# q and k laid out by the host with the dims on the partitions: attention followed by two MLPs

## Chip, core and metric

The kernel runs on one core of a Trainium2 chip, in one launch. The metric is device time in microseconds (us): the time of the run on the chip, as the median of several runs. Engines are named as in the profile: PE is TensorE (matmuls), DVE VectorE, ACT ScalarE, POOL GpSimd, SP the engine that issues most DMAs. Arrays are float32 in the chip's memory (HBM), except the MLP weights, which are float64.

## The reference

B = 4 batches, H = 8 heads, S = 576 positions, D = 64 dims per head. q and k are turned by rope, attention is a full softmax per head, and the result, 2304 tokens of 512, goes through two MLPs.

```python
def rotate(x):                                   # x: [B, H, S, 64]; cos, sin: [S, 32]
    x1, x2 = x[..., :32], x[..., 32:]
    return concatenate([x1 * cos - x2 * sin, x1 * sin + x2 * cos], axis=-1)
scores = matmul(rotate(q), rotate(k).transpose(0, 1, 3, 2)) / sqrt(64)
attn = exp(scores - max(scores)); attn = attn / (sum(attn) + 1e-9)
x = matmul(attn, v).transpose(0, 2, 1, 3).reshape(2304, 512)
x = (sigmoid(x @ w_gate) * (x @ w_val)) @ w_out              # hidden dim 1536
h = x @ w2_in                                                # hidden dim 2048
out = (h * sigmoid(1.702 * h)) @ w2_out
```

## The kernel before

**Pairs, tiles, slots.** Two heads make a pair: 16 pairs, p0 to p15. A head has four tiles of 128 queries and a tail of 64; the two tails share a tile, so a pair has nine units of scores (even units the first head, odd ones the second, the ninth both tails). The program is written out in slots, one unit of scores each (`slot`, from line 586), in a fixed order on every engine. Slot 9i holds the first scores of pair i. Each other stage of a pair comes a fixed number of slots ahead of 9i (`LOAD`, `ROPE_MUL`, `ROPE_ADD`, `ROPE_T`) or behind it (`PT`, `PV`, the normalisation). In a slot the order is: scores, splits left from the slot before (`later`), products with V, transposes of P, loads, normalisation, rope, exponential, a step of weight decoding. Each engine works its own list in order and waits where an operand or a buffer isn't ready.

**q and k.** `load` brings q and k of a pair with the positions on the partitions (x: four positions to a partition, then the tails). Rope multiplies by a sine table with the halves of the dims swapped and by a cosine table (six products on POOL, `rope_mul`), and adds on DVE (`rope_add`). `transpose_qk` turns nine blocks of 128x128 on PE into PSUM, in three groups. Of each group ACT takes a rounded high part X (type float32r, which PE multiplies fast) and DVE the rest Y = x - X. Both are [64 dims of two heads, 1152 columns of q and k]. `stack` then moves halves with six DMAs on SP, so that the high and low parts of one head lie on the 128 partitions: X and Y belong to the first head, Z and Zs to the second. The fifth and sixth of them overwrite what the first four read, so SP waits for those to land. The scores of a unit (`scores`) are two matmuls per half of the keys, which sum the exact products of the parts. p0 does its stacking on ACT and DVE straight from PSUM (`stack_first`).

**After the scores.** DVE takes the row maximum, ACT the exponential and its sum, DVE the reciprocal, POOL multiplies P by it. PE transposes P (41 blocks a pair, `transpose_p`; PSUM tiles of one tag, three buffers, shared with `transpose_qk`), ACT or DVE bring the blocks to SBUF, PE multiplies with V (`pv`), and the result is split into high and low parts for the MLPs. V and P keep the interleaved order of positions, so the output rows come out in runs with a step of four, and `out2` stores each tile with one or more DMAs (`row_runs`), on SP and in the last block partly on POOL.

**The MLPs** follow with all tokens on chip. The float64 weights are decoded to float32 by integer operations on DVE, with one operation on ACT and one on POOL per piece. The first chunk is decoded during the attention, one operation a slot, from unit 4 of p3 on. The later ones go beside the MLP matmuls.

Of the kernel before, what the change touches and what calls it, by code (L numbers as in the profile page):

```python
# [8 lines left out]
F32 = mybir.dt.float32  # L9
# [13 lines left out]
# bits 0x0feffe00: the high word of float32's largest numbers, after the scaling  # L23
# [8 lines left out]
def attention_then_mlps(  # L32
    ctx: ExitStack,
    tc: tile.TileContext,
    q: bass.AP,
    k: bass.AP,
# [6 lines left out]
    cos_t: bass.AP,  # L43
    sin_t: bass.AP,
# [4 lines left out]
    B, H, S, D = q.shape  # L49
    NT, DM = out.shape  # L50
    FF1 = w_gate.shape[1]
# [97 lines left out]
    npairs = B * NPAIR  # L149
# [10 lines left out]
    def load(i):  # L160
        b, hp = divmod(i, NPAIR)
        hs = slice(2 * hp, 2 * hp + 2)
        x = rp.tile([P, 2, NCHK, D], F32, tag="x", name="x", bufs=2)
        # first head: k main | k tail, q tail | q main; second: q main | q tail, k tail | k main
        main = lambda src, h: src[b, h, 0:MAIN, :].rearrange("h (p c) d -> p h (c d)", p=P)
        nc.sync.dma_start(
            out=x.rearrange("p h c d -> p (h c d)")[:, (MAINC + 1) * D : (3 * MAINC + 1) * D].rearrange(
                "p (h n) -> p h n", h=2
            ),
            in_=main(q, hs),  # L170
        )
        for h, c, pq in ((0, 0, TAIL), (1, MAINC + 1, 0)):
            nc.sync.dma_start(
                out=x[:, h : h + 1, c : c + MAINC, :].rearrange("p h c d -> p h (c d)"),
                in_=main(k, slice(2 * hp + h, 2 * hp + h + 1)),
            )
            for src, p in ((q, pq), (k, TAIL - pq)):
                nc.sync.dma_start(out=x[p : p + TAIL, h, MAINC, :], in_=src[b, 2 * hp + h, MAIN:S, :])
        st[i] = dict(x=x, P={})
        st[i]["nm"] = sp.tile([P, 2, 5], F32, tag="nm", name="nm", bufs=4)  # L180
        st[i]["sum"] = sp.tile([P, 9], F32, tag="sum", name="sum", bufs=4)

    def load_v(i):
        b, hp = divmod(i, NPAIR)
        vt = sp.tile([P, 2 * MAINC + 1, D], F32, tag="v", name="v", bufs=3)
        for h in range(2):
            nc.sync.dma_start(out=vt[h * TAIL : (h + 1) * TAIL, 2 * MAINC, :], in_=v[b, 2 * hp + h, MAIN:S, :])
        nc.sync.dma_start(
            out=vt[:, 0 : 2 * MAINC, :].rearrange("p (h c) d -> p h (c d)", h=2),
            in_=v[b, 2 * hp : 2 * hp + 2, 0:MAIN, :].rearrange("h (p c) d -> p h (c d)", p=P),  # L190
        )
        st[i]["v"] = vt

    def rope_mul(i, n, eng=nc.gpsimd):
        x = st[i]["x"]
        if n == 0:
            st[i]["xr"] = rp.tile([P, NCHK, 2, D], F32, tag="xr", name="xr", bufs=2)
        t = st[i]["xr"]
        h, n = divmod(n, 3)
# [12 lines left out]

    def transpose_qk(i, g):
        """q and k with the dims of both heads on the partitions, in exact hi and lo parts; columns
        [k main | k tail | q tail | q main] of the first head, [q main | q tail | k tail | k main]
        of the second."""
        xr = st[i]["xr"]
        if g == 0:
            for n in ("X", "Y", "Z"):
                st[i][n] = rp.tile([P, NCHK * P], F32R, tag=n, name=n, bufs=2)  # L220
            st[i]["Zs"] = rp.tile([P, S], F32R, tag="Zs", name="Zs", bufs=2)
        g0, g1 = ((0, 3), (3, 6), (6, 9))[g]
        ps = ps_t.tile([P, 512], F32, tag="pt", name="ps_qk", bufs=3)
        n = (g1 - g0) * P
        for ch in range(g0, g1):
            nc.tensor.transpose(  # L226
                ps[:, (ch - g0) * P : (ch - g0 + 1) * P], xr[:, ch].rearrange("p h d -> p (h d)"), ident
            )

        c = slice(g0 * P, g1 * P)  # L230
        X, Y, Z, Zs = (st[i][n_] for n_ in ("X", "Y", "Z", "Zs"))

        def split():
            hi, lo = X[:, c], Y[:, c]
            nc.scalar.activation(hi, ps[:, :n], AF.Copy)
            nc.vector.tensor_tensor(lo, ps[:, :n], f(hi), ALU.subtract)
            if g == 2:
                stack(i)

        if i:  # L240
            later.append(split)
        return ps[:, :n], c
# [50 lines left out]
    def exps(i, u):  # L293
        """Rows of P: exp(s - max), unnormalised, and their sums."""
# [31 lines left out]
    # the groups of P transposed that DVE takes out of PSUM, and not ACT; those of the first pair  # L326
# [75 lines left out]
    def split_mm(ps, l, r, n):  # L402
        """Sum of n products of exactly split operands: hi*hi + hi*lo + lo*hi."""
# [29 lines left out]
    row_runs = []  # L433
    for t in range(NT // P):
        runs = []
        c = 0
        while c < P:
            b, j = divmod(t * P + c, S)
            if j < MAIN:
                ch, p0 = divmod(j, P)  # L440
                n = min(P - c, P - p0)
                runs.append((c, n, b * S + MAINC * p0 + ch, MAINC))
            else:
                n = min(P - c, S - j)
                runs.append((c, n, b * S + j, 1))
            c += n
        row_runs.append(runs)

# [23 lines left out]
    def out2(c, nchunk, W, n, g):  # L472
        if c == 0:
            new_acc(n)
        for t in range(width[n] // P):
# [7 lines left out]
            if c == nchunk - 1:  # L483
                for x, (o, m, row, step) in enumerate(row_runs[n * BLK // P + t]):
# [217 lines left out]
```

## Time and profile before

| | |
|---|---|
| time, median of 3 runs | 1165.64 us (1165.47 to 1167.69) |
| span of the profiled execution | 1165.3 us; what lies around the span isn't listed |
| busy: PE, DVE, ACT, POOL | 1134.9, 766.2, 426.1, 327.1 us |
| first matmul of scores | 15.84 us |
| first matmul of an MLP | 323.3 us |
| read from HBM, written to it | 50.46 MB, 4.72 MB |

PE busy means that a matmul is in its pipeline, so matmuls overlap and their own durations add up to more than their share; the chain of waits gives each only what it adds. PEld is PE's weight load, SPq the issue of a DMA by SP. A row with "x3" stands for three instructions merged.

### The profile page before, as it was taken

Reading aid. Unit: us, or ns where it says so; the run is one execution under the profiler, and the core shown is the slowest. Engines: PE = TensorE matmul, PEld = TensorE weight load, DVE = VectorE, ACT = ScalarE, POOL = GpSimd, SP = SyncE. Lnnn points to the kernel's source line nnn. Section 1 sums busy time; section 2 is a strip of 40 time slices with the busy share of each in tenths; the row PEclk is TensorE's granted clock in tenths of the full one; section 3 lists DMA queues with packets and bytes.
Section 4 is the critical chain, followed back from the end, with each engine's and each line's share of the span. In section 5 each row is a group of like instructions: output and inputs, shape, how many; then the busy total and the mean of one; then the engine's idle time right before and its main releaser. Section 6 shows DMA issues by size and latency. Waiting matters only on the chain.

```text
span 1165.3 us, 16369 instructions
## 1 busy us (share of the span) xinstructions
PE 1134.9 (97%) x6096; PEld 917.3 (79%) x6096; DVE 766.2 (66%) x1388; ACT 426.1 (37%) x952; POOL 327.1 (28%) x333
## 2 busy tenths in 40 slices
PE   3999999999999999999999999999999999999998
PEld 2776666777688888888888888888888888888886
DVE  6879999777544555555655555567667676676744
ACT  3776777777621211211212112332323223232221
POOL 6768787765300010100101002331001010010100
PEclk9999999999999999999999999999999999999999
DMA  4555655453211111111111111011111111111014
GB/s 128 123 147 145 150 136 138 110 124 84 66 37 37 37 55 37 55 37 37 55 37 55 37 37 36 20 37 55 37 37 55 37 55 37 37 55 37 19 37 126
DMA packets 46063, 76.15 MB, mean 65 GB/s; under 512 B 11728, under 2 KB 24016, under 8 KB 45984
## 3 DMA queue, kind: packets, MB, share of 16 engines
q1 hardware_dynamic: 45696, 74.19, 23.3%
q8 instruction: 48, 0.79, 0.3%
q0 software_dynamic: 288, 0.92, 0.2%
q14 instruction: 31, 0.25, 0.1%
HBM read 50.46 MB, written 4.72 MB: 47 GB/s over the span
## 4 chain that ended last, share of the span: by engine, by line
PE 90%; DMA 3%; DVE 2%; ACT 2%; issue 1%; SPq 1%; POOL 1%; POOLq 0%; DVEq 0%
PE psh L406 42%; PE pso L406 29%; PE ps_x L377 6%; PE ps_p L347 4%; PE pss L287 3%; PE pss L288 3%; DMA Zs<-X 2%; PE ps_qk L226 1%; DMA X<-Y 1%; ACT P L305 1%; DVE r L318 0%; ACT PT L334 0%; SPq L266 0%; DVE xr L211 0%; DVE nm L290 0%
## 5 line engine op out<-in xcount | busy, mean ns | idle before, releaser
L406 PE MATMUL psh<-xhl,w_in 128*128 128x512 f32 (+1 forms) x2400 | 504.2, 368 | 0.0
L406 PEld LDWEIGHTS psh<-xhl,w_in 128*128 128x128 f32 x2400 | 419.3, 188 | 76.1 <-issue 0.5
L420 ACT ACTIVATE sg<-psh 128x512 f32<-128x512 f32 (+1 forms) x140 | 77.5, 554 | 367.5 <-PE psh L406 366.8
L406 PE MATMUL pso<-w_out,g 128*128 128x512 f32 x864 | 202.4, 389 | 0.0
L422 DVE TENSOR_TENSOR gf<-psh,sg 128x512 f32<-128x512 f32 (+1 forms) x140 | 88.9, 635 | 158.7 <-PE psh L406 111.9
L406 PEld LDWEIGHTS pso<-w_out,g 128*128 128x128 f32 x864 | 161.7, 188 | 33.2
L423 ACT ACTIVATE g<-gf 128x512 fp32r<-128x512 f32 (+1 forms) x140 | 82.5, 590 | 242.0 <-DVE gf L422 242.0
L138 POOL TENSOR_TENSOR w_in<-wt,w_in 128x512 fp32r<-128x512 f32 x40 | 51.7, 1292 | 389.0 <-DVE w_in L137 389.0
L424 DVE TENSOR_TENSOR g<-gf,g 128x512 fp32r<-128x512 f32 (+1 forms) x140 | 95.3, 681 | 91.7 <-ACT g L423 91.7
L406 PE MATMUL pso<-g,w_out 128*128 128x512 f32 (+1 forms) x720 | 152.8, 368 | 0.0
L406 PEld LDWEIGHTS pso<-g,w_out 128*128 128x128 f32 x720 | 125.8, 189 | 22.6
L290 DVE TENSOR_REDUCE nm<-pss 128x1 f32<-128x576 f32 x144 | 108.0, 750 | 49.0 <-PE pss L288 48.3
L322 POOL TENSOR_SCALAR P<-P,r 128x576 f32<-128x576 f32 x128 | 106.4, 844 | 84.9 <-DVE r L319 47.9
L138 POOL TENSOR_TENSOR w_out<-wt,w_out 128x512 fp32r<-128x512 f32 x28 | 36.1, 1290 | 264.0 <-DVE w_out L137 264.0
L377 PE MATMUL ps_x<-PT,v 128*64 128x256 f32 (+3 forms) x640 | 105.3, 425 | 3.3 <-DVE xhl L396 3.3
L305 ACT ACTIVATE P<-pss,nm 128x576 f32<-128x576 f32 x128 | 95.5, 746 | 26.6 <-DVE nm L290 24.6
L334 ACT ACTIVATE PT<-ps_p 128x384 f32<-128x384 f32 (+2 forms) x193 | 77.7, 435 | 59.4 <-PE ps_p L347 43.7
L482 DVE TENSOR_TENSOR acc<-pso,acc 128x512 f32<-128x512 f32 x126 | 83.1, 685 | 20.3 <-PE pso L406 18.0
L347 PE MATMUL ps_p<-ident,P 128*128 128x128 f32 x576 | 84.5, 279 | 1.1 <-POOL P L322 0.9
L347 PEld LDWEIGHTS ps_p<-ident,P 128*128 128x128 f32 x576 | 65.8, 141 | 24.7 <-issue 20.0
L467 DVE TENSOR_TENSOR acc<-pso,acc 128x512 f32<-128x512 f32 (+1 forms) x100 | 61.6, 634 | 28.8 <-PE pso L406 28.8
L377 PEld LDWEIGHTS ps_x<-PT,v 128*64 128x64 f32 (+1 forms) x640 | 35.8, 134 | 31.8 <-issue 20.4
(59 smaller groups left out, 1035.4 us busy)
## 6 DMA issues: line engine op xcount, KB each, us to landing
raw<-in_moe_w_out_dram SPq DMA_DIRECT2D x28, 512.0 KB, 3.5
raw<-in_moe_w_in_dram SPq DMA_DIRECT2D x16, 512.0 KB, 3.6
raw<-in_moe_w_gate_dram SPq DMA_DIRECT2D x12, 512.0 KB, 3.8
raw<-in_moe_w_val_dram SPq DMA_DIRECT2D x12, 512.0 KB, 3.8
Z<-X SPq DMA_DIRECT2D x15, 288.0 KB, 3.1
Z<-Y SPq DMA_DIRECT2D x15, 288.0 KB, 3.9
X<-Y SPq DMA_DIRECT2D x15, 288.0 KB, 3.0
x<-in_q_dram SPq DMA_DIRECT2D x16, 256.0 KB, 3.0
```

The costliest lines, as they stand in the source:

```text
L138: lambda: nc.gpsimd.tensor_tensor(w[:, 1, :], f(t), f(w[:, 0, :]), ALU.subtract),
L290: nc.vector.tensor_reduce(nm, ps[:, :, :HALF], axis=AX.XY, op=ALU.max, negate=True)
L305: nc.scalar.activation(st[i]["P"][j][:, c : c + S].rearrange("p (n c) -> p n c", n=2), ps[:, :, :HALF], AF.Exp, bias=nm, accum_out=st[i][" ...
L322: nc.gpsimd.tensor_scalar(pt, pt, r[:, c - a : c - a + 1], 1.0, op0=ALU.mult, op1=ALU.mult)
L334: nc.scalar.activation(dst, src, AF.Copy)
L347: nc.tensor.transpose(ps[:, t * P : (t + 1) * P], pt[:, (3 * g + t) * P : (3 * g + t + 1) * P], ident)
L377: nc.tensor.matmul(ps[h * D : (h + 1) * D, :n], vt[r, vc, :], PT[r, pc, :], start=(t == 0), stop=(t == MAINC))
L406: nc.tensor.matmul(ps, l(sl, a), r(sr, a), start=(sl == 1 and a == 0), stop=(sl + sr == 0 and a == n - 1))
L422: nc.vector.tensor_tensor(gf, pss[-1][:, :wd], sg, ALU.mult)
L423: nc.scalar.activation(g[:, 0, m, :], gf, AF.Copy)
L424: nc.vector.tensor_tensor(g[:, 1, m, :], gf, f(g[:, 0, m, :]), ALU.subtract)
L482: nc.vector.tensor_tensor(a, ps[:, :DM], a, ALU.add)
```

## The change

The host (where arrays are only laid out, and tables of the shapes alone are made) now gives q and k as one array: per pair 128 partitions (64 dims of the first head, 64 of the second) by 1152 columns, and once more with the two halves of each head's dims swapped. Columns are, for the first head, k main, k tail, q tail, q main, and for the second q main, q tail, k tail, k main: the order that X, Y, Z had. "HALVES" 0 and 1 are the columns 0 to 575 and 576 to 1151. cos and sin come in the same layout, [128, 2, 1152]. v comes in tiles as the kernel holds them. Positions keep their natural order, so each output tile of 128 rows is stored by one DMA. The MLPs don't change.

```diff
-    def load(i):                # 7 DMAs: q main of both heads; per head k main, q tail, k tail
-    def load_v(i):              # 3 DMAs, 3 buffers
-    def rope_mul(i, n, eng=nc.gpsimd):   # 6 per pair: 4 of [128, 9x32], 2 of [128, 9x64]
-    def rope_add(i, h):
-    def transpose_qk(i, g):
-    def stack_first(h):
+    HALVES = (slice(0, S), slice(S, 2 * S))
+    def load(i, c=slice(0, 2 * S)):
+        if i not in st:
+            st[i] = dict(P={}, x=rp.tile([P, 2 * S], F32, tag="x", name="x", bufs=2))
+        nc.sync.dma_start(out=st[i]["x"][:, c], in_=qk[i, 0, :, c])
+    def load_swapped(i, n, c=slice(0, S)):
+        if ("xs", n) not in st[i]:
+            st[i]["xs", n] = rp.tile([P, S], F32, tag="xs", name="xs", bufs=3)
+        nc.sync.dma_start(out=st[i]["xs", n][:, c], in_=qk[i, 1, :, n * S + c.start : n * S + c.stop])
+    def load_v(i):
+        vt = sp.tile([P, 2 * MAINC + 1, D], F32, tag="v", name="v", bufs=2)
+        nc.sync.dma_start(out=vt, in_=v[i])
+    def mul(i, swapped, n, eng, c=slice(0, S)):
+        c_ = slice(n * S + c.start, n * S + c.stop)
+        t = st[i]["xs", n][:, c] if swapped else st[i]["x"][:, c_]
+        eng.tensor_tensor(t, t, cos_sin[:, swapped, c_], ALU.mult)
+    def add(i, n, c=slice(0, S)):
+        x = st[i]["x"][:, n * S + c.start : n * S + c.stop]
+        nc.vector.tensor_tensor(x, x, st[i]["xs", n][:, c], ALU.add)
+    def rope_mul(i, n):
+        mul(i, 1 - n % 2, n // 2, nc.gpsimd)
+    def rope_add(i, n):
+        add(i, n)
+    def split_qk(i, n):
+        if n == 0:
+            new_pair(i)                       # tiles X, Y, Z, Zs, nm, sum
+        c = HALVES[n]
+        x, hi, lo = (st[i][n_][:, c] for n_ in ("x", "X", "Y"))
+        nc.scalar.activation(hi, x, AF.Copy)
+        nc.vector.tensor_tensor(lo, x, f(hi), ALU.subtract)
+        if n == 1:
+            stack(i)
+    def first_pair():
+        k, q = HALVES
+        q0, q1 = slice(S, S + TAIL + P), slice(S + TAIL + P, 2 * S)
+        lo, hi = slice(0, D), slice(D, P)
+        first, others = slice(0, TAIL + P), slice(TAIL + P, S)
+        for c, n, c_ in ((k, 0, slice(0, S)), (q0, 1, first), (q1, 1, others)):
+            load(0, c)
+            nc.scalar.dma_start(out=cos_sin[:, :, c], in_=cos_sin_t[:, :, c])
+            load_swapped(0, n, c_)
+        load(1)
+        load_swapped(1, 0)
+        nc.gpsimd.dma_start(out=ident, in_=ident_t)
         ...
+        def rope(c, n, c_, eng):
+            mul(0, 0, n, nc.vector, c_)
+            mul(0, 1, n, eng, c_)
+            add(0, n, c_)
+            hi_of(X[lo, c], x[lo, c])         # hi_of: ACT copy; rest: DVE subtraction
+        rope(k, 0, slice(0, S), nc.gpsimd)
+        rope(q0, 1, first, nc.vector)
+        rest(X[hi, k], x[lo, k], X[lo, k])
+        hi_of(Y[hi, q0], x[lo, q0])
+        rest(X[hi, q0], x[lo, q0], X[lo, q0])
+        nc.vector.tensor_copy(Y[lo, q0], f(X[hi, q0]))
+        rope(q1, 1, others, nc.gpsimd)
+        hi_of(Zs[hi], x[hi, k])
+        hi_of(Y[hi, k], x[hi, q])
+        hi_of(Z[lo, k], x[hi, k])
+        hi_of(Z[lo, q], x[hi, q])
+        rest(Z[hi, k], x[hi, k], Zs[hi])
+        rest(Z[hi, q], x[hi, q], Y[hi, k])
+        nc.vector.tensor_copy(Zs[lo], f(Z[hi, k]))
+        rest(X[hi, q1], x[lo, q1], X[lo, q1])
+        nc.vector.tensor_copy(Y[lo, q1], f(X[hi, q1]))
+        hi_of(Y[hi, q1], x[lo, q1])
     ...
     def out2(c, nchunk, W, n, g):
         ...
-                for x, (o, m, row, step) in enumerate(row_runs[n * BLK // P + t]):
-                    (nc.gpsimd if x and n == NBLK - 1 else nc.sync).dma_start(...)
+                row = n * BLK + t * P
+                nc.sync.dma_start(out=out[row : row + P, :], in_=a)
     ...
-    LOAD, LOAD_V = 27, 13
-    ROPE_MUL = {ANY: (20, 20, 18, 19, 19, 15), 1: (22, 21, 18, 14, 17, 14), 2: (22, 20, 16, 22, 18, 17)}
-    ROPE_ADD = {ANY: (13, 11), 1: (15, 14), 2: (11, 11)}
-    ROPE_T = {ANY: (8, 7, 6), 1: (9, 9, 7), 2: (10, 9, 7)}
+    LOAD, LOAD_V = 25, -1
+    LOAD_S = {ANY: (20, 18)}
+    ROPE_MUL = {ANY: (17, 19, 15, 14)}
+    ROPE_ADD = {ANY: (12, 11), 1: (8, 7)}
+    SPLIT = {ANY: (8, 7), 1: (6, 5)}
     ...
     def step_scores(G):
         if 0 <= G < NU * npairs:
             scores(*divmod(G, NU))
-        if G == 0:
-            stack_first(1)
     def step_rope(G):
-        for fn, table in ((rope_mul, ROPE_MUL), (rope_add, ROPE_ADD), (transpose_qk, ROPE_T)):
+        for fn, table in ((rope_mul, ROPE_MUL), (rope_add, ROPE_ADD), (split_qk, SPLIT)):
     ...
     def step_load(G):
         ...
+        for i, n in due(G, LOAD_S, -1):
+            if (i, n) not in ((0, 0), (0, 1), (1, 0)):
+                load_swapped(i, n)
     ...
     with tc.manual_schedule():
-        load(0)
         ...
-        stack_first(0)
+        first_pair()
```

The split is now called in the rope step of its slot and no longer in the slot behind it. `stack`, `scores` and all stages behind them stay as they were.

## Rows read from the trace of the kernel before

**Rows 1.** The page, busy time of each engine, its share and instructions.
```profile
PE 1134.9 (97%) x6096; PEld 917.3 (79%) x6096; DVE 766.2 (66%) x1388; ACT 426.1 (37%) x952; POOL 327.1 (28%) x333
```

**Rows 2.** Stretches: bounds, length, busy PE, PEld, DVE, ACT, POOL, granted clock, DMA share, GB/s.
```profile
15.84:37.88 22.04, 15.39 (x82) 13.32 (x82) 17.89 (x30) 13.33 (x31) 15.30 (x15) 0.92 0.50 123
37.88:55.29 17.41, 16.98 (x121) 11.25 (x119) 15.59 (x32) 11.96 (x33) 12.99 (x16) 1.00 0.47 113
...
91.82:110.80 18.98, 18.25 (x133) 12.89 (x133) 17.55 (x37) 14.06 (x38) 15.46 (x17) 1.00 0.57 146
...
186.78:205.84 19.06, 18.21 (x133) 12.89 (x133) 17.29 (x34) 13.22 (x37) 15.54 (x18) 1.00 0.48 117
...
242.28:260.50 18.22, 18.22 (x133) 12.90 (x133) 13.96 (x31) 13.12 (x37) 12.90 (x16) 1.00 0.52 123
...
278.70:296.60 17.90, 17.90 (x132) 12.81 (x132) 11.98 (x29) 12.82 (x36) 6.30 (x10) 1.00 0.42 92
```

**Rows 3.** Chain of waits through a plain pair: start, us, what.
```profile
229.16 0.48 PE ps_qk L226 x3
229.64 0.14 PE pss L287
...
231.42 0.33 PE ps_qk L226 x3
...
232.72 0.58 PE ps_x L377 x4
233.30 0.33 PE pss L287
```

**Rows 4.** Instructions on tile ps_qk: count, ns min/median/max, first and last start.
```profile
L235 ACT ACTIVATE X<-ps_qk x45: 478/480/495, 22.5 to 287.3; 128x384 fp32r<-128x384 f32 x45
L236 DVE TENSOR_TENSOR Y<-ps_qk,X x45: 540/547/558, 23.4 to 287.8; 128x384 fp32r<-128x384 f32 x45
```

**Rows 5.** Instructions on tile x, the same columns.
```profile
L211 DVE TENSOR_TENSOR xr<-x,xr x32: 747/900/1334, 9.3 to 275.1; 128x576 f32<-128x576 f32 x32
```

**Rows 6.** Groups by line and shape, whole span: busy us, mean ns, idle before.
```profile
L203 POOL TENSOR_TENSOR xr<-x,sin_sb 128x288 f32<-128x288 f32 x62 | 53.4, 882 | 4.9 <-DMA x<-in_k_dram 4.9
L207 POOL TENSOR_TENSOR x<-x,cos_sb 128x576 f32<-128x576 f32 x30 | 43.9, 1464 | 0.2
...
L252 ACT ACTIVATE Y<-X 64x576 fp32r<-64x576 f32 x1 | 0.7, 682 | 0.0
```

**Rows 7.** Groups on DVE from 91.82 to 205.84 (p4 to p9).
```profile
L290 DVE TENSOR_REDUCE nm<-pss 128x1 f32<-128x576 f32 x54 | 40.4, 747 | 7.2 <-PE pss L288 7.1
```

**Rows 8.** Timeline of the start: start us, us, engine, line, what.
```profile
0.74 0.44 SPq L166 DMA_DIRECT2D x<-in_q_dram  x1
...
7.19 0.83 DVE L203 TENSOR_TENSOR xr<-x,sin_sb 128x288 f32<-128x288 f32 x2 [7.19 <-DMA x<-in_k_dram]
...
15.84 0.61 PE L287 MATMUL pss<-X 128*128 128x288 f32 x1 [0.52 <-DVE X L250]
```

**Rows 9.** One stretch of the start, columns as in rows 2.
```profile
2.00:8.00 6.00, 0.00 (x0) 0.00 (x0) 0.81 (x2) 0.02 (x1) 1.29 (x3) 1.00 0.91 273
```

**Rows 10.** Chain of waits into the first scores of p5.
```profile
100.93 0.57 DVE Y L236
...
107.72 2.95 DMA X<-Y
...
110.80 0.37 PE pss L287
```

**Rows 11.** The page, DMA issues: count, KB each, median us to landing.
```profile
x<-in_q_dram SPq DMA_DIRECT2D x16, 256.0 KB, 3.0
...
out_dram<-acc SPq DMA_DIRECT2D x18, 128.0 KB, 2.3
```

**Rows 12.** Chain of waits at the end.
```profile
1159.10 0.70 DVE acc L482
...
1161.42 0.57 POOLq L698
```

More of the change, by code (lines that the diff above doesn't have):

```diff
@@ L34, in attention_then_mlps @@
     tc: tile.TileContext,
-    q: bass.AP,
-    k: bass.AP,
+    qk: bass.AP,
     v: bass.AP,
@@ L48, in attention_then_mlps @@
     nc = tc.nc
-    B, H, S, D = q.shape
+    npairs, _, _, S = qk.shape
+    S //= 2
+    D = v.shape[3]
     NT, DM = out.shape
+    B, H = NT // S, DM // D
     FF1 = w_gate.shape[1]
@@ L158, in run_later @@
             fn()
-    def load(i):
[L161 to L179, printed above, removed]
+    HALVES = (slice(0, S), slice(S, 2 * S))
@@ L180, in load @@
         st[i]["nm"] = sp.tile([P, 2, 5], F32, tag="nm", name="nm", bufs=4)
         st[i]["sum"] = sp.tile([P, 9], F32, tag="sum", name="sum", bufs=4)
+        for n in ("X", "Y", "Z"):
+            st[i][n] = rp.tile([P, 2 * S], F32R, tag=n, name=n, bufs=2)
+        st[i]["Zs"] = rp.tile([P, S], F32R, tag="Zs", name="Zs", bufs=2)
     def load_v(i):
[L184 to L187, printed above, removed]
@@ L209, in rope_add @@
-    def rope_add(i, h):
-        xr = st[i]["xr"][:, :, h, :]
-        nc.vector.tensor_tensor(xr, st[i]["x"][:, h], xr, ALU.add)
-    def transpose_qk(i, g):
[L217 to L242, printed above, removed]
@@ new lines, in rope_add @@
+    def rope_add(i, n):
+        add(i, n)
+    def split_qk(i, n):
+        if n == 0:
+            new_pair(i)
[17 more added lines that the diff above has]
+        nc.gpsimd.dma_start(out=ident, in_=ident_t)
+        new_pair(0)
+        x = st[0]["x"]
+        X, Y, Z, Zs = (st[0][n] for n in ("X", "Y", "Z", "Zs"))
+        hi_of = lambda dst, src: nc.scalar.activation(dst, src, AF.Copy)
+        rest = lambda dst, src, h: nc.vector.tensor_tensor(dst, src, f(h), ALU.subtract)
+        def rope(c, n, c_, eng):
[20 more added lines that the diff above has]
+        hi_of(Y[hi, q1], x[lo, q1])
@@ L432, in attention_then_mlps @@
     acc = {}
[L433 to L447, printed above, removed]
     def new_acc(n):
@@ L595, in attention_then_mlps @@
     with tc.manual_schedule():
-        load(0)
-        nc.gpsimd.dma_start(out=sin_sb, in_=sin_t)
-        nc.gpsimd.dma_start(out=cos_sb, in_=cos_t)
-        nc.gpsimd.dma_start(out=ident, in_=ident_t)
-        load(1)
-        for n in range(6):
-            rope_mul(0, n, nc.vector if n in (0, 1, 2, 5) else nc.gpsimd)
-            if n == 2:
-                rope_add(0, 0)
-        rope_add(0, 1)
-        st[0]["qk"] = [transpose_qk(0, g) for g in range(3)]
-        stack_first(0)
+        first_pair()
         wts[1, 0] = Weights(1, 0)
@@ L646, in attention_then_mlps, with _columns, _layout @@
         pend[0](*pend[1:])
-_INS = ["q", "k", "v", "moe_w_gate", "moe_w_val", "moe_w_out", "moe2_w_in", "moe2_w_out"]
+_INS = ["moe_w_gate", "moe_w_val", "moe_w_out", "moe2_w_in", "moe2_w_out"]
+def _columns(x, y, h):
+    import numpy as np
+    n = MAINC * P
+    return np.concatenate([x[:n], x[n:], y[n:], y[:n]] if h == 0 else [y[:n], y[n:], x[n:], x[:n]])
+def _layout(q, k, v):
+    import numpy as np
+    B, H, S, D = q.shape
+    qk = np.stack(
+        [
+            np.concatenate([_columns(k[b, 2 * p + h], q[b, 2 * p + h], h).T for h in range(2)])
+            for b in range(B)
+            for p in range(H // 2)
+        ]
+    )
+    halves = qk.reshape(-1, 2, 2, D // 2, 2 * S)
+    qk = np.stack([qk, halves[:, :, ::-1].reshape(qk.shape)], axis=1)
+    n = MAINC * P
+    vp = v.reshape(B * H // 2, 2, S, D)
+    main = vp[:, :, :n].reshape(-1, 2, MAINC, P, D).transpose(0, 3, 1, 2, 4).reshape(-1, P, 2 * MAINC, D)
+    tail = vp[:, :, n:].reshape(-1, P, 1, D)
+    return qk, np.concatenate([main, tail], axis=2)
 def _tables(S, D):
@@ L663, in _tables @@
     scale = np.float32(1.0 / math.sqrt(D))
-    out = []
-    for t in (cos, sin):
-        main = t[: MAINC * P].reshape(P, MAINC, D)
-        tail = t[MAINC * P :]
-        a = np.zeros((P, 2 * MAINC + 1, D), np.float32)
-        a[:, :MAINC] = main * scale
-        a[:TAIL, MAINC] = tail * scale
-        a[TAIL:, MAINC] = tail
-        a[:, MAINC + 1 :] = main
-        out.append(a)
-    return out[0], out[1], np.eye(P, dtype=np.float32)
+    tables = [np.concatenate([_columns(t, t * scale, h).T for h in range(2)]) for t in (cos, sin)]
+    return np.stack(tables, axis=1), np.eye(P, dtype=np.float32)
 def kernel(**inputs):
@@ L686 @@
     arrays, args = {}, []
-    named = [(n, inputs[n]) for n in _INS] + list(zip(("cos", "sin", "ident"), _tables(S, D)))
+    named = list(zip(("qk", "v"), _layout(*(_np.asarray(inputs[n]) for n in ("q", "k", "v")))))
+    named += [(n, inputs[n]) for n in _INS] + list(zip(("cos_sin", "ident"), _tables(S, D)))
     for name, a in named:
```

48 lines of the change are left out of this document (3 added, 45 removed).

## The prediction

> **What bounds the kernel now.** I read the page's busy shares first: TensorE (PE) is busy 97% of the span [rows 1]. A share over the whole span says nothing about the attention, which the change touches, so the next view was the table of stretches, cut at the first matmul of each pair's scores [rows 2]. There are 16 pairs of heads, p0 to p15, and nine slots to a pair. The reader is to see three kinds of stretch.
> - p0 takes 22.0 us with PE busy for 15.4: the pipeline fills, and waits decide.
> - Plain pairs (p2, p3, p10 to p14) take 18.2 us and PE is busy for all of it. There every microsecond taken off PE's order of work shortens the pair.
> - Six pairs, p4 to p9, in which weights are decoded, take 19.0 us on average (91.82 to 205.84). PE's work is the same 18.25 us, but VectorE (DVE) is busy for 17.5 in the first of them and 17.3 in the last, and PE idles 0.7 and 0.85 [rows 2]. Of DVE's own idle time in them, 7.1 us in six pairs, 1.2 each, is waiting for scores from PE [rows 7].
>
> From p1 to p14 the pairs average (296.60-37.88)/14 = 18.48 us. Behind 323.3 us the MLPs run from PE with nothing of the change in them but the last stores. The chain of waits through a plain pair consists of PE alone, and shows what the transposes of q and k cost there [rows 3].
>
> **The change, part by part.**
>
> *The nine transposes of a pair go.* They sit in three groups of three. On the chain two groups take 0.48 us, behind a product with V, and one takes 0.33, behind a transpose of P: 1.29 us [rows 3]. Not all comes back. The 0.15 more of the first two is a change of operand shape, and a score that follows a product with V directly shows 0.33 instead of 0.14 [rows 3], 0.19 more. With the groups gone, the scores of two slots follow such a product. I take 1.29-2x0.19 = 0.91 us a pair. The ends are 0.72 (the switch paid behind all three) and 1.29 (never). The groups for p1 to p15 ran in the stretches of p0 to p14.
> - Seven plain pairs: 7x0.91 = 6.4 us.
> - p1 had 0.43 us of idle PE and otherwise the same work: 0.9 us.
> - Six decoding pairs: PE falls to 17.3 us, so DVE is next. Its own work stays, and of its 1.2 us of waiting for PE some 0.5 must remain, because scores, maximum, exponential and the next scores follow each other. I take 0.7 us each, 4.2 in all; ends 0 and 1.3.
>
> *The split reads SBUF instead of PSUM.* ScalarE: 3x0.480 = 1.44 us becomes two activations of 576 columns, nearest row 0.682: 1.36, nothing either way [rows 4, 6]. DVE: three subtractions of 0.547, 1.64 us, from PSUM [rows 4], become two of 576 with both inputs in SBUF. The nearest row is the rope's addition, 0.747 to 1.334 us with 0.900 in the median [rows 5]: 1.5 to 2.7, I take 1.8. The 0.16 more lies under PE in plain pairs and is inside the 0.7 of the others. Below 1.5 nothing speaks for a gain.
>
> The spread of [rows 5] against the constant 540 to 558 ns of [rows 4] is a contention, and a page bears on it: the Trainium skill, "SBUF — State Buffer", "Who interferes with whom", says that a VectorE instruction with two SBUF inputs contends with a GpSimd instruction that reads SBUF and that the later one waits for the whole of the other. The rows agree. By that rule at its worst the sum would be that of rival B.
>
> *Rope.* GpSimd (POOL) did four half products of 0.882 and two full ones of 1.464 a pair [rows 6]: 6.46 us. Now it does four of 576 contiguous columns, 5.86. The 0.6 us is no term: POOL is not the bound (12.9 of 18.2 us) [rows 2]. The two additions on DVE stay.
>
> *Loads.* Per pair seven issues for x and three for v become one for x (0.59 MB), two for the half-swapped copy (0.29 MB each) and one for v; SP has six issues fewer, 0.44 us for one like them [rows 8]. Bytes grow by 0.59 MB a pair. The DMA engines are at half load in plain pairs (0.52) [rows 2], so this is hidden unless a load stands in front of something due. It does so in one place, below. The swapped halves come three slots (5.7 us) ahead of their product, a 0.25 MB load lands in 3.0 [rows 11], and v comes nine slots ahead: nothing.
>
> *The added wait.* The load of x for pair i+2 is issued in slot 9i-7. It reuses the buffer that pair i's second split reads in that same slot, so SP waits there for DVE. Behind it in SP's queue stand the six stacking transfers of pair i, without which its scores can't start. They need the same split, so the wait costs them nothing, but the load's issue (0.44) and its transfer (0.59 MB at 273 GB/s [rows 9], 2.2 us) go ahead of them. Stacking takes 9.2 us from the end of the split (101.50) to the end of its last transfer (110.67), 0.13 us before the scores [rows 10]: they waited for it there. Now the chain is 9.2+2.6 = 11.8 us, and the split stands two slots earlier: seven slots of 1.92 us less about one for the split itself leave 12 to 13.5. I take nothing; the upper end is the load landing whole first, rival D.
>
> *The first pair.* Before, x was there at 7.19 us and the first scores ran at 15.84, behind rope, nine transposes and a split [rows 8]. Now the k half needs x, its swapped copy and cos and sin: 1.18 MB from 2.0 us on at 273 GB/s [rows 9], at 6.3; with part of the next pieces between, 6.8. Then a product on POOL (1.46), an addition (0.90), three DVE operations on 192 columns (0.30 each), the low part of k (0.90) and of those 192 (0.30): first scores at 11.3 us, 4.5 earlier. The other head's operands come from ten more operations on DVE and ScalarE before its first maximum. From the first scores to p1's took 22.0 us. There pair 1's splits move to slots 3 and 4 with x of pair 3 loaded ahead of its stacking, POOL waits for x of pair 2 (whose buffer the first pair frees late) in front of its first normalisation, and in return PE has some nine transposes fewer, at a clock that averaged 0.92. I take 22.5, so p1 starts 4.0 us earlier. Ends: 0, if the fill gives all of it back; 8, if the second head's earlier start comes through.
>
> *The stores.* Rows are in order now, one SP transfer a tile, where the last tile had a second one issued by POOL at 1161.42, after a sum begun at 1159.10 and a further one [rows 12]. A store lands in 2.3 us [rows 11]; the last issue moves forward a little: 0.5 us, ends 0 and 1.5.
>
> Sum: 4.0 + 0.9 + 6.4 + 4.2 + 0.5 = 16.0 us off the profiled execution's span of 1165.3 (what lies around it isn't shown), which stands 0.3 below the median of the runs: 1149.3+0.3 = 1149.6 us. The ends add up to 0+8x0.72+0+0 = 5.8 and 8+8x1.29+6x1.3+1.5 = 27.6: 1159.8 to 1138.0.
>
> **The rivals.**
> - A, the forecast: 1149.6.
> - B, DVE takes the decoding pairs. If both new subtractions wait for POOL as the worst addition did, they cost 2x1.334-1.64 = 1.0 us more a pair [rows 4, 5], and 17.6+1.0+0.6 = 19.2 us is a decoding pair: 0.2 us slower each instead of 0.7 faster. 1149.6+6x0.9 = 1155.0. For it: DVE is busy for some 92% of these pairs. Against it: the median row.
> - C, everything shortens. Stacking starts earlier, p4 to p9 lose their idle PE too, and the fill passes on the second head's gain: 8+8x1.1+6x1.1+1.0 = 24.4, 1141.2. For it: [rows 10] show stacking as the last wait in such a pair. Against it: DVE there.
> - D, slower: the load of x in front of the stacking decides. Scores start a chain C after the split, and the split ends some 2.5 slots (4.8 us) into the pair, so a pair takes 4.8+C. It bounds PE from C = 12.5 on. From C = 14.0 it takes back the start and the tail (18.8 against 18.48, over 14 pairs). C is 11.8; were the load to land whole first (3.0 for 0.25 MB [rows 11], 1.3 for the rest) it would be 13.9, and with one more us of sharing about 15.0: 14x(19.8-18.48) = 18.5, less 4.5, is 14.0 slower, 1179.6. For it: stacking was already just in time. Against it: 11.8 is the rows' sum.
> - E: what PE is spared becomes waiting in every pair and the start is given back: about 1165.6. PE fully busy in the plain pairs speaks against it.
>
> **How the numbers follow.** A 63%, B 13%, C 13%, D 8%, E 3%. A measurement of this kernel can't tell less than 0.2%, 2.3 us, from no change. A to C are faster by more: 0.89; same 0.03; slower 0.08. The range takes in the ends of the unknown costs and with them B and C: 1138 to 1160. D, E and what of C goes deeper are left out.
>
> **What would show it.** Right: plain pairs at 17.3 us with PE still busy throughout; decoding pairs at 18.3 with DVE at 95% or more; first scores near 11.3 and p1's near 34; no row of ps_qk. Wrong: plain pairs that idle PE before the first scores of a pair, released by the last stacking transfer (D); subtractions averaging over 1.2 us (B); p1 at 37 or later. The prediction as a whole is wrong if the plain pairs don't get shorter.

## The result: slower, by 0.8%

The kernel after is 10 us slower where 16 us of gain were forecast. This section shows where the time went, the experiments look for the cause, and the part behind them says which steps of the prediction failed.

| | before | after | forecast |
|---|---|---|---|
| median, us (before: run beside after) | 1165.8 | 1175.9 | 1149.6 |
| ratio to before, 95% interval | | 1.0081 [1.0069, 1.0093] | |
| span of the profiled execution | 1165.3 | 1174.0 | 1149.3 |
| p1's first scores (the fill) | 37.88 | 44.09 | 33.9 |
| p1 | 17.3 | 19.3 | 16.4 |
| p2, p3 | 36.6 | 37.0 | 34.8 |
| p4 to p9 (weights decoded) | 114.0 | 117.0 | 109.8 |
| p10 to p13 | 72.9 | 71.8 | 69.2 |
| p14 | 18.2 | 17.3 | 17.3 |
| p15 and all behind it | 868.5 | 867.4 | 868.0 |

The lower seven rows add up to the span, a pair lasting from its first scores to the next pair's. The loss has two places: the fill (+6.2 us) and p1 to p14 (+3.5 in all). From the forecast they are 10.2 and 15.0 us away. (p15's first scores start at 296.83 in before, and not at 296.60 as [rows 2] have it, so p14 took 18.2 us there and not 17.9.)

The spans differ by 8.7 us and the medians by 10.1. Where one execution's time and span both stand on record, the time is 1.7 to 1.9 us longer; by that the profiled execution of before took some 1167.1 us (an estimate), 1.3 more than the median. Its fill seems to be the reason: 22.04 us, where e3 below, with the same program up to slot 18, has 20.87. So the change's loss in the fill is rather 7 to 8 us than 6.2 (an estimate).

### The profile after

The page's busy times, which answer to [rows 1]: PE is busy 8.3 us less, and the span is 8.7 us longer.

```profile
PE 1126.6 (96%) x5952; PEld 904.9 (77%) x5952; DVE 774.3 (66%) x1374; ACT 425.9 (36%) x938; POOL 329.3 (28%) x299
```

The stretches, with the columns of [rows 2]: the fill, p1, p4, p9, p11, p12 and p14.

```profile
12.92:44.09 31.17, 15.51 (x69) 12.70 (x70) 23.40 (x33) 14.88 (x33) 19.60 (x16) 0.97 0.41 115
44.09:63.40 19.31, 18.67 (x111) 11.91 (x112) 12.97 (x27) 11.64 (x31) 11.81 (x12) 0.87 0.53 144
...
100.45:120.19 19.74, 17.63 (x124) 12.06 (x124) 17.99 (x36) 14.04 (x39) 15.84 (x15) 1.00 0.63 170
...
197.87:217.40 19.53, 17.68 (x123) 12.06 (x124) 16.44 (x33) 13.52 (x39) 16.41 (x16) 1.00 0.55 146
...
235.88:253.62 17.74, 17.59 (x123) 12.06 (x124) 14.67 (x30) 12.35 (x33) 12.70 (x13) 1.00 0.58 161
253.62:271.66 18.04, 17.63 (x124) 12.08 (x124) 14.65 (x30) 13.34 (x37) 13.69 (x15) 1.00 0.57 157
...
289.24:306.56 17.32, 17.32 (x126) 12.00 (x124) 11.91 (x28) 12.91 (x36) 7.02 (x10) 1.00 0.42 95
```

Behind p1, PE's work fell in every pair, from about 18.2 to 17.6 us, but PE now idles: 2.1 us in p4, 1.9 in p9, 0.4 in p12. From p14 on no x is left to load ahead of a pair's stacking; its scores and p15's come 3 us after the last transfer has landed, and p14, the last stretch above, is filled to the end. The next fence is the chain of waits from p10's end through p11, which answers to [rows 3, 10].

```profile
226.97 5.62 DMA Zs<-X
...
232.66 3.08 DMA X<-Y
235.74 0.14 issue
235.88 0.37 PE pss L290
...
238.90 0.69 ACT X L208
239.59 0.02 issue
239.62 1.46 DVE Y L209
241.07 0.67 DVE nm L293
...
241.84 0.84 ACT P L308 x2
242.68 0.04 issue
242.72 0.40 PE pss L290
```

p11's scores begin 0.14 us after the last stacking transfer lands. The fourth one, Zs<-X, lasted 5.62 us, and SP's timeline for the next pair shows why (start, length of the issue):

```profile
242.70 0.33 SPq L167 DMA_DIRECT2D x<-in_qk_dram  x1
243.07 0.47 SPq L269 DMA_DIRECT2D Z<-X  x1
243.58 0.60 SPq L269 DMA_DIRECT2D Z<-Y  x1
...
245.44 1.40 SPq L269 DMA_DIRECT2D Zs<-X  x1
249.61 0.46 SPq L269 DMA_DIRECT2D Y<-X  x1
250.38 0.46 SPq L269 DMA_DIRECT2D X<-Y  x1
```

The load of x waits for the second subtraction, which ended at 242.67, and goes 0.03 us later, with the stacking right behind it. From there to the landing of X<-Y (253.48) it is 10.8 us; over p2 to p13 the chain measures 10.8 to 12.0, mean 11.4, against 8.3 to 9.5 before. The split itself ends 6.8 us into p11 (7.6 to 8.1 into the decoding pairs).

### The profile page after: what moved, and what is told of

It reads as the page before. It is cut to its first block, busy times and chain, and to the rows that moved or that the text cites. A ratio compares the mean times of both kernels' runs of the same rounds, so it can differ in the third digit from the quotient of the medians.

```text
span 1174.0 us, 15872 instructions
## 1 busy us (share of the span) xinstructions
PE 1126.6 (96%) x5952; PEld 904.9 (77%) x5952; DVE 774.3 (66%) x1374; ACT 425.9 (36%) x938; POOL 329.3 (28%) x299
## 4 chain that ended last, share of the span: by engine, by line
PE 80%; DMA 8%; DVE 6%; SPq 2%; issue 1%; ACT 1%; POOL 0%; DVEq 0%; ACTq 0%; POOLq 0%
PE psh L409 42%; PE pso L409 29%; DMA Zs<-X 5%; PE ps_x L380 3%; DMA X<-Y 3%; PE ps_p L350 2%; PE pss L290 2%; DVE Y L209 2%; SPq L269 2%; DVE nm L293 2%; PE pss L291 1%; ACT P L308 1%; DMA xs<-in_qk_dram 0%; DVE x L194 0%; DVE PT L335 0%
## 5 line engine op out<-in xcount | busy, mean ns | idle before, releaser
L325 POOL TENSOR_SCALAR P<-P,r 128x576 f32<-128x576 f32 x128 | 116.8, 924 | 74.8 <-DVE r L322 56.5
L290 PE MATMUL pss<-X 128*128 128x288 f32 (+3 forms) x176 | 53.7, 331 | 33.2 <-DVE X L231 12.9
L350 PEld LDWEIGHTS ps_p<-ident,P 128*128 128x128 f32 x576 | 66.2, 142 | 24.6 <-issue 17.6
```

The source lines that it names most:

```text
L325: nc.gpsimd.tensor_scalar(pt, pt, r[:, c - a : c - a + 1], 1.0, op0=ALU.mult, op1=ALU.mult)
L350: nc.tensor.transpose(ps[:, t * P : (t + 1) * P], pt[:, (3 * g + t) * P : (3 * g + t + 1) * P], ident)
```

## The experiments

Each was compared with the kernel before on the same chip; "a pair's chain" is the time from the end of its last subtraction to the landing of X<-Y.

**e1: no bytes ahead.** Loads of x for pairs 2 and up bring 64 of 1152 columns, into two fixed tiles; the rest of q and k is left out.

```diff
-            load(i)
+            load(i, slice(0, 64))
```

> The changed kernel, with the load of x of pairs 2 to 15 cut to its first 64 of 1152 columns (it leaves out the rest, so those pairs work on old values; x lies in two fixed tiles). In the changed kernel the stacking of a pair took 10.8 to 12.0 us from the end of the split to its last landing and the pair's first scores came 0.14 us behind that, from p1 to p13. Theory 1 (the load of x, in front of the stacking in SP's queue, holds every pair): the chain falls to 8.0 to 8.6 us, the slack before the first scores opens, plain pairs take 17.3 us, decoding pairs 18.3, and the time is 1157 to 1162 us. Theory 2 (the two new subtractions from SBUF, blocked by POOL, and ScalarE's longer list hold the pairs): pairs stay at 18.0 to 19.5 us and the time stays above 1170.

1162.4 us, 0.9973 [0.9961, 0.9985]. Chains 7.5 to 8.7, landing 2.1 to 3.2 us before the scores from p2 on; plain pairs 17.62, decoding ones 18.6 to 19.1 (both above what was expected), p1's start 39.15. So it is the load. Whether its bytes or its wait, e1 can't tell: its 64 columns are read by the first subtraction alone, so it is issued before the second one ends (229.17), and Z<-X, which needs only ScalarE's X, goes early too.

```profile
227.60 0.33 SPq L168 DMA_DIRECT2D x<-in_qk_dram  x1
228.04 0.47 SPq L270 DMA_DIRECT2D Z<-X  x1
229.19 0.46 SPq L270 DMA_DIRECT2D Z<-Y  x1
```

e12 adds bytes without such a wait.

**e2: the load behind the stacking.** Nothing left out.

```diff
-    LOAD, LOAD_V = 25, -1
+    LOAD, LOAD_V = 24, -1
```

> The changed kernel with LOAD 24 for 25: x of pair i+2 is issued behind the six stacking transfers of pair i, not in front. Theory 1: the chain from split to last landing falls from 11.5 to 8.0 to 8.6 us; x itself comes 6 us later, so POOL may wait 1 to 2 us for it; pairs of 17.3 to 18.3 us, time 1158 to 1165. Theory 2: 1170 or more.

1166.9 us, 1.0011 [1.0001, 1.0022], more than the 1158 to 1165 expected. From p2 on the chains are 7.6 to 8.5, p1 to p14 take 254.1 us instead of 262.5, the plain pairs 17.62; p12's stretch:

```profile
244.25:261.89 17.64, 17.60 (x126) 12.08 (x124) 14.66 (x30) 13.07 (x36) 13.43 (x14) 1.00 0.61 165
```

One slot gives 8.4 us back. p1 still starts at 42.73 after a chain of 11.6: the load for p3 still stands ahead of its stacking, which in this pair comes two slots later than in the others.

**e3: the kernel before, transposes one slot earlier.** The doubt was whether [rows 10] show the bound of the kernel before in all its pairs, since most began their scores 0.14 us after X<-Y landed.

```diff
-        ANY: (8, 7, 6),
+        ANY: (9, 8, 7),
```

> The kernel before, with its three groups of transposes of q and k one slot earlier (9, 8, 7 for 8, 7, 6), and so its splits and its stacking. In it the last stacking transfer landed 0.14 us ahead of the first scores in 11 of 15 pairs, though PE showed as busy throughout. Theory 3 (the pairs of the kernel before were held by the stacking too, and the busy PE hid it): slack opens and plain pairs fall from 18.2 to 17.9 us or less, time 1159 to 1162. Rival (PE's work itself took the 18.2 us, as the prediction read it): plain pairs stay at 18.2, only decoding pairs may gain 0.3 us, time 1163 to 1166.

1162.7 us, 0.9974 [0.9965, 0.9984]. In p11 to p14 the transfer now lands 2.0 to 2.6 us early and the pairs still take 18.3 (p12's stretch below), so PE bounded them, as predicted; the transfer that landed just in time wasn't the limit. Decoding pairs gain 3.2 us in all. The fill's 1.2 us can't be the edit's, as the program up to slot 18 is that of before.

```profile
237.36:255.64 18.28, 18.26 (x134) 12.87 (x133) 14.14 (x31) 13.12 (x37) 12.89 (x15) 1.00 0.51 122
```

**e4: GpSimd without the four products of pair 1** (left out) in the kernel after.

```diff
-        mul(i, 1 - n % 2, n // 2, nc.gpsimd)
+        if i != 1:
+            mul(i, 1 - n % 2, n // 2, nc.gpsimd)
```

> The changed kernel without POOL's four rope products of pair 1 (left out, so that pair is wrong). In the changed kernel these ran on POOL from 11.0 to 17.2 us while DVE worked on the first pair, and DVE's subtractions, cast, product and addition there took 1.3 to 1.7 us each instead of 0.35 to 0.75. Theory 4 (they block DVE's SBUF reads): these operations fall to 0.3 to 0.8 us, the second head's first scores come at 15 to 16.5 us instead of 20.8 and p1's 4 to 5 us earlier than 44.1. Rival (DVE waits for its data): 20 to 21 us as before, p1 unchanged.

1171.0 us, 1.0043 [1.0027, 1.0059]. DVE's timeline in the fill, in the kernel after, and under it POOL's:

```profile
9.97 2.90 DVE L231 TENSOR_TENSOR X<-x,X 64x576 fp32r<-64x576 f32 x2
12.90 1.34 DVE L244 CAST Y<-X 64x192 fp32r<-64x192 f32 x1
14.28 1.66 DVE L190 TENSOR_TENSOR x<-x,cos_sin 128x384 f32<-128x384 f32 x1
16.04 1.57 DVE L194 TENSOR_TENSOR x<-x,xs 128x384 f32<-128x384 f32 x1
...
21.70 0.75 DVE L293 TENSOR_REDUCE nm<-pss 128x1 f32<-128x576 f32 x1
```
```profile
11.04 1.62 POOL L190 TENSOR_TENSOR x<-x,cos_sin 128x576 f32<-128x576 f32 x1 [0.25 <-DMA x<-in_qk_dram]
12.62 2.90 POOL L190 TENSOR_TENSOR xs<-xs,cos_sin 128x576 f32<-128x576 f32 x2
15.48 1.71 POOL L190 TENSOR_TENSOR x<-x,cos_sin 128x576 f32<-128x576 f32 x1
```

The same instructions of DVE in e4:

```profile
10.34 1.82 DVE L232 TENSOR_TENSOR X<-x,X 64x576 fp32r<-64x576 f32 x2
12.19 0.26 DVE L245 CAST Y<-X 64x192 fp32r<-64x192 f32 x1
12.48 0.56 DVE L190 TENSOR_TENSOR x<-x,cos_sin 128x384 f32<-128x384 f32 x1
13.14 0.56 DVE L194 TENSOR_TENSOR x<-x,xs 128x384 f32<-128x384 f32 x1
...
17.78 1.41 DVE L294 TENSOR_REDUCE nm<-pss 128x1 f32<-128x576 f32 x2
```

While POOL multiplies, each DVE operation lasts about as long as one of POOL's, 1.3 to 1.7 us; without that, 0.26 to 0.9. The second head's first scores run at 16.85 instead of 20.76, and p1 starts at 40.05, 4.0 us earlier. In between stands POOL's queue: x of pair 2 comes 4.1 us earlier, and so does the first normalisation (23.67 instead of 27.80). As POOL is also spared the products themselves, e4 alone doesn't show what the blocking costs; e6 takes that up.

**e5: e2, and the load for p3 two more slots later**, behind p1's stacking too.

```diff
-        i, u = divmod(G + LOAD, NU)
-        if u == 0 and 1 < i < npairs:
-            load(i)
+        for i in range(2, npairs):
+            if G == NU * i - (22 if i == 3 else LOAD):
+                load(i)
```

> The kernel after with every load of x one slot later (behind the six stacking transfers of its pair, as in e2) and x of pair 3 two more slots later, so that it stands behind the stacking of p1 too. Theory (the load of x in front of the stacking costs 3 us wherever it stands): p1's chain from the end of the split to the last stacking transfer falls from 11.6 to about 8, p1 starts some 3.3 us earlier than in e2 (39 to 40 us against 42.7), the pairs behind are as in e2 (plain 17.6, decoding 18.6 to 19.4), the time is 1163 to 1164. Rival (the first pair's pace is set by VectorE and GpSimd alone, and the chain is hidden there): p1 still starts at 42 or later, the time is that of e2, 1166.9.

1163.9 us, 0.9985 [0.9976, 0.9994]. p1's chain is 7.6, its start 39.95. The theory holds: the other 2.8 us of the load.

**e6: e5, and one copy of the fill on GpSimd.**

```diff
-        nc.vector.tensor_copy(Y[lo, q1], f(X[hi, q1]))
+        nc.gpsimd.tensor_copy(Y[lo, q1], f(X[hi, q1]))
```

> e5, and the last copy of the first pair's first head (low part of q to the other half of the partitions) is made by GpSimd and no longer by VectorE, so that GpSimd can't begin the four products of pair 1 before VectorE is nearly through with the first pair. Theory (those products block VectorE's two-input operations and casts in SBUF between 11 and 17 us): the copies and subtractions of the second head take 0.3 to 0.8 us each instead of 1.3 to 1.7, the second head's first scores run at 16 to 17.5 us instead of 20.8, p1 starts at 36 to 37, the time is 1158.5 to 1161. Rival (something else holds up p1, so that what VectorE gains is waited away: GpSimd's products of pair 1 end later now, and p1's split needs them): p1 starts at 39 or later, 1163 or more.

1163.5 us, 0.9977 [0.9964, 0.9989], with p1 at 39.37: the rival. The first half of the theory held: the copies and subtractions of the second head take 0.46 to 0.76 us, its first scores run at 16.06 (20.55 in e5). But that gain is waited away: GpSimd's products of pairs 1 and 2, moved back, now run until 26.6, ahead of its first normalisation (see e11).

**e7: e2, GpSimd without the products of pairs 6 to 11** (left out).

```diff
-        mul(i, 1 - n % 2, n // 2, nc.gpsimd)
+        if not 6 <= i <= 11:
+            mul(i, 1 - n % 2, n // 2, nc.gpsimd)
```

> e2 without GpSimd's four rope products of pairs 6 to 11 (left out; the additions and all else stay), which ran in the stretches of p4 to p10. Theory (in the decoding pairs VectorE is the bound, and part of its time is waiting for GpSimd at the port: integer operations and subtractions with both inputs in SBUF): the pairs p5 to p9 fall from 18.6 to 18.0 or below, the new subtraction there averages 0.75 to 0.85 us instead of 1.1, the time is 1162 to 1164. Rival (VectorE's own work alone is the bound, as the prediction read it): these pairs stay at 18.4 or more and the time within 1 us of e2's 1166.9.

1158.1 us, 0.9930 [0.9913, 0.9948], a larger gain than expected. One decoding pair of e2, then one of e7:

```profile
171.60:190.29 18.69, 17.66 (x125) 12.08 (x124) 17.92 (x36) 13.55 (x36) 16.46 (x14) 1.00 0.63 179
```
```profile
114.46:131.88 17.42, 17.42 (x125) 12.06 (x124) 16.34 (x36) 13.55 (x37) 10.01 (x10) 1.00 0.68 192
```

As many instructions of DVE (36) take 1.6 us less, and the pair becomes PE's. The same operation, the addition of 1e-9 to two sums, from 112 to 205 us in e2 and in e7:

```profile
L321 DVE TENSOR_SCALAR r<-sum 128x2 f32<-128x2 f32 x20 | 14.4, 719 | 1.2 <-ACT P L308 1.2
```
```profile
L322 DVE TENSOR_SCALAR r<-sum 128x2 f32<-128x2 f32 x21 | 7.1, 340 | 0.0
```

PE's longest waits in e2, over the same time, were for exponentials (5.6 us), and these waited for DVE's maxima (11.3); POOL itself waited for DVE (12.0). So it isn't POOL's own list that holds the pair: waiting for GpSimd, and not DVE's own work, made DVE the bound there.

**e8: the kernel before with its loads of x three slots later**, in front of the stacking in SP's order.

```diff
-    LOAD, LOAD_V = 27, 13
+    LOAD, LOAD_V = 24, 13
```

> The kernel before with its seven loads of x three slots later (LOAD 24 instead of 27), which puts them, 0.59 MB as well, directly in front of the six stacking transfers; layout and transposes are those of before. Theory (it is the place of the load in the queue, not the new layout, that lengthened the chain): from the end of the split to the last stacking transfer 11.5 to 12.5 us instead of 8.2 to 9.4, the scores wait for it in every pair from p1 to p13, plain pairs 20 to 22 us instead of 18.2, the time 1190 to 1215; p14, with no load ahead, stays at 18.2. Rival (the longer chain belongs to the new layout, its larger pieces or its traffic): chain under 9.5, time 1162 to 1168.

1167.8 us, 1.0016 [1.0006, 1.0026]; chains 8.4 to 10.0, plain pairs 18.2: a miss. The last of the seven issues goes 3.95 us before the first stacking transfer, which waits for the split:

```profile
231.23 1.22 SPq L178 DMA_DIRECT2D x<-in_k_dram  x1
235.18 0.48 SPq L266 DMA_DIRECT2D Z<-X  x1
```

These loads find a free buffer (in that layout rope's additions write to another tile), and all seven have landed by 234.10. The order in the queue alone costs the plain pairs nothing (p1 and p4 took 2.0 and 0.9 us more than in before's profile, why stays open); what is left is that in the kernel after the load waits for the same subtraction as the stacking, and starts with it. e12 tries that.

**e9: e5 without the addition of 1e-9.**

```diff
-        nc.vector.tensor_scalar_add(r, s[:, a:b_], 1e-9)
-        nc.vector.reciprocal(r, r)
+        nc.vector.reciprocal(r, s[:, a:b_])
```

> e5 without VectorE's addition of 1e-9 to the sums, five a pair; the reciprocal reads the sums directly. (A sum is at least 1, its largest term is exp(0), so in float32 the addition changes no bit.) Theory (in the decoding pairs this small operation, 0.07 us by itself and 0.72 on average in e2, waits for GpSimd's whole instruction, and that wait is what makes VectorE the bound there): VectorE gets 2 us or more back in each decoding pair, they fall from 18.65 to 17.5 to 17.8 with PE busy throughout, plain pairs stay at 17.6, the time is 1156.5 to 1158.5. Rival (the wait only moves to VectorE's next operation that needs the port, the subtraction or a decoding operation): decoding pairs at 18.3 or more, the time 1161 to 1164.

1160.8 us, 0.9956 [0.9943, 0.9968]. (The 0.07 us of the expectation is what the addition adds to a chain; its shortest duration on two sums is 0.15.) In the decoding pairs the rival holds: 18.8, as the wait moved on to the subtraction (1.14 us on average) and a decoding operation (1.43). The plain pairs fell to 17.38, which wasn't expected; at the place in a plain pair where PE waited in e2, the chains of e2 and then of e9 show

```profile
250.86 0.23 PE ps_p L357
251.09 0.04 issue
251.13 0.40 PE pss L290
```
```profile
247.83 0.23 PE ps_p L356
248.06 0.25 PE pss L290
```

The scores waited 0.04 us for an exponential, and their first matmul then cost 0.40 instead of 0.25: 0.19 of the 0.24 us.

**e10: the kernel before with e3's and e9's edits.**

> The kernel before with the transposes one slot earlier (as e3) and without the same addition: what the same two repairs bring with the old layout. Theory: there PE's 18.25 us is the bound as soon as VectorE is relieved, so the decoding pairs fall from about 18.5 to 18.25 and the plain ones stay at 18.2 to 18.3; the time is 1160.5 to 1162, and e9, with the new layout, is 3 to 5 us faster than this one. Rival (the new layout brings nothing once both are repaired): this one within 1.5 us of e9.

1163.9 us, 0.9981 [0.9972, 0.9990]; plain pairs 18.28 as expected, decoding ones 18.64 and the time above what was expected: no better than e3. e9 is 3.1 us faster, at the low end of what was expected.

**e11: e9, e6's copy, and pair 2's products later.**

```diff
-    ROPE_MUL = {ANY: (17, 19, 15, 14)}
-    ROPE_ADD = {ANY: (12, 11), 1: (8, 7)}
+    ROPE_MUL = {ANY: (17, 19, 15, 14), 2: (14, 14, 12, 12)}
+    ROPE_ADD = {ANY: (12, 11), 1: (8, 7), 2: (10, 9)}
```

> e9, with e6's copy on GpSimd, and with the four products of pair 2 four slots later on average (14, 14, 12, 12 slots ahead instead of 17, 19, 15, 14; its additions 10, 9 instead of 12, 11). Theory (in e6 GpSimd's queue set p1's start: two products of pair 2, the first waiting for its load, stood in front of the first normalisation): the first normalisation runs at 23 to 24 us instead of 26.6, p1 starts at 35.5 to 37.5 instead of 39.4, the time is 1153 to 1156. Rival (the products of pair 2 now collide with p1's stacking or its own split, or VectorE is the next bound in the fill): p1 starts at 39 or later, 1157 or more.

1157.3 us, 0.9924 [0.9911, 0.9936], above the 1153 to 1156 expected. The first normalisation starts at 23.57, p1 at 35.70, as the theory has them. It is the fastest of the kernels that compute everything, before and after among them, though the addition it drops is no part of the change.

**e12: the kernel before with one extra transfer** that starts with the stacking.

```diff
         for dst, src in (...):
             nc.sync.dma_start(out=dst, in_=src)
+            if src is first and i + 2 < npairs:      # first = Y[D:P], the second transfer
+                xr = st[i]["xr"].rearrange("p n h d -> p (n h d)")
+                nc.sync.dma_start(out=xr, in_=q[0, 0:4].rearrange("h (a s) d -> (h a) (s d)", a=32))
```

> The kernel before with one transfer of 0.59 MB from HBM added for p1 to p13, behind the second of the six stacking transfers, so that like the load of x in the kernel after it starts once the split has ended and goes ahead of the last four (it overwrites a tile of rope's that nobody reads any more; 7.7 MB more traffic in all). Theory (a transfer that starts with the stacking costs 3 us, whatever the layout; in e8 the loads were issued 5 us earlier and so cost nothing): chain 11 to 12 us instead of 8.2 to 9.4, scores wait for it in p1 to p13, these pairs 20 to 21.5 us instead of 18.2 to 19, p14 at 18.2, the time 1188 to 1206. Rival (transfers side by side don't hold each other up at this load): chain under 9.5, the time 1164 to 1168.

1219.9 us, 1.0461 [1.0441, 1.0480]. From p2 to p13 the chains are 10.9 to 12.4, as the theory has them, p1's 10.1, p14's 8.3. As this transfer waits for nothing of its own, its bytes are enough to lengthen the chain, by some 3 us. But p2 to p12 take 21 to 24 us, more than expected. The stretch p11 of e12, and lines of its chain, in which a matmul of scores takes 0.24 us and later 0.13:

```profile
263.15:286.92 23.77, 21.00 (x133) 15.08 (x133) 13.51 (x31) 13.42 (x36) 12.84 (x16) 0.86 0.46 119
```
```profile
260.01 3.01 DMA X<-Y
...
263.15 0.58 PE pss L291
263.73 0.24 PE pss L292
...
269.71 0.13 PE pss L292
```

PE idled before these scores. The granted clock of the stretch averages 0.86, and PE's busy time is 21.0 us where p14 has 18.2: 2.8 us on top of the wait.

## Why the prediction was wrong

*"The added wait": the step that failed in the pairs.* It was taken at nothing, and cost 8.4 us over p1 to p14 (e2 against after). What decided is where the chain starts: "seven slots of 1.92 us less about one for the split itself" were to leave 12 to 13.5 us, and 10.7 are left. The split ends 6.8 us into a plain pair and 7.8 on average into a decoding one; rival D had 4.8. ScalarE and VectorE run behind PE's slot: in the chain above the first copy of X starts 3.0 us into p11, and its subtraction (1.46 us, as a product of POOL ran from 239.04 to 240.46) and a maximum come ahead of the second subtraction. 6.8+10.8+0.14 is p11's 17.74; 7.8+11.5+0.14 is the decoding pairs' 19.5. So D's mechanism decided, from C = 17.6-6.8-0.14 = 10.7 on and not from 12.5; its 1179.6 overstated the plain pairs, 19.8 against 18.0. e12 shows the cost itself, with the layout and the transposes of before. The start was taken from slots of the program. The rows of before gave a first hint: a split that was written for the slot beginning 4x18.98/9 = 8.4 us into p4 ended at 101.50, 9.7 us into it, 1.3 behind [rows 2, 10]. In the kernel after it is 2.9 behind (slot 2 begins 3.9 us into p11), which no row of before shows.

The chain was forecast at 11.8 us and measures 11.4 on average, which is partly luck: without the load it is 7.6 (e2) and not 9.2, and the load costs 3.8 and not 2.6. That "the wait costs them nothing" doesn't hold either: Z<-X needs only ScalarE's X and goes 1.4 us before the subtraction ends in e2 (232.05 and 233.44), while in the kernel after it stands behind the load. How the 3.8 divide between wait and bytes no run separates in this layout; in the old one the bytes cost some 3 (e12).

*"The first pair": 10.2 us off.* The first scores come at 12.9 (forecast 11.3; 11.4 to 13.0 over all kernels with this head), but the fill from there to p1 took 31.2 instead of 22.5. The load of x for p3 ahead of p1's stacking, which the prediction named and put inside the 22.5, lengthens p1's chain from 8.22 to 11.55; taking it away gave 2.8 (e5 against e2). Leaving out POOL's products of pair 1 gave 4.0 (e4), by the blocking of DVE and by POOL's shorter queue; the blocking alone gave 0.6 of p1's start (e6 against e5), as POOL's queue then decided. Pair 2's products ahead of the first normalisation, which the prediction named without a price, were that queue: 39.37 in e6, 35.70 in e11. So the three don't add up. With all of them removed, and the addition of 1e-9, it is 24.1 from the first scores to p1 (e11), 1.6 from the forecast. The prediction had priced neither DVE's waiting for POOL in the fill nor POOL's queue.

*The nine transposes.* Mechanism right, size nearly. p14, free of the load, gained 0.87 us; e9 against e10, with nothing late in either, 18.28-17.38 = 0.90, the forecast 0.91. In e2 p10 to p13 gained 0.59 each; the rest went to the late exponential that e9 shows. In after they kept 0.26.

*Decoding pairs.* Forecast 18.3, measured 19.5, and 18.75 without the load (e5). "DVE: two subtractions ... I take 1.8" was undersized: they average 1.14 us there, 2.3 the two. Rival B's mechanism exists, but priced as subtractions alone it missed where most of it lies: e7's 1.3 us a pair, with POOL's products gone, come from every DVE operation that the products hold up. The Trainium skill, "SBUF — State Buffer", "Who interferes with whom", which the prediction weighed for two-input operations, counts copies, casts and tensor_scalar operations too, where they run in a two-port mode. Which mode ours ran in no trace shows, but the rows agree: a tensor_scalar of 0.15 us at its shortest took 0.72 on average in e2, and a cast of 0.26 us (e4) took 1.34.

*The stores.* 1.05 us, forecast 0.5, inside its bounds.

*From span to time.* The step "which stands 0.3 below the median of the runs" set one execution's span against the median of others. With the 1.7 to 1.9 us that lie between span and time, the same sum gives some 1151 us, too small a difference to matter here.

Left open: how much of the fill is left to win, and whether POOL's products can be placed in the decoding pairs so that DVE doesn't meet them; neither was tried.

## What to carry to other kernels

Look at what a prefetch waits for, not only where it is queued: one that reuses a buffer whose last reader also releases a latency-critical transfer starts together with it, and here lengthened the chain by 3 to 4 us; a slot later it was free. Take the moment at which a stage really ends from the trace of its engine, not from the slot it is written in, before adding a chain to it. And a transfer that lands just before its reader starts isn't proof that it is the bound: e3 moved it away by 2 us and the plain pairs stayed as they were.

## What the runs showed of the hardware

A wait of PE can cost more than its length: p1 of after ran at a granted clock of 0.87, with PE busy for 18.67 us, where it took 16.84 at 1.00 in e5 (1.8 of the 2.9 us by which p1 missed its forecast), and p11 of e12 paid 2.8 us in this way. The same matmul form added 0.24 us to the chain behind the wait (1.2 GHz) and 0.13 later (2.4 GHz).

On the chains above and in [rows 3], the first matmul of scores after a product with V adds 0.33 us, one after an idle gap of 0.04 us 0.40, one after a transpose of the last, narrower P 0.25, and one after a full-width transpose 0.14.
